# A transformer block on one core: scale before shift, values in partitions by head, probabilities copied by DMA, batched aggregation, and a new order

## The chip, the cores and the metric

The kernel runs on one core of a Trainium2 chip. The metric is the device time of one execution in microseconds; the median of some runs is given. PE is the matmul engine (PEld its weight loads), DVE the vector engine, ACT the scalar engine, POOL GpSimd; SP issues most DMAs. Each engine takes its instructions in program order.

## The reference

One batch, S = 2048 rows, D = 512, 32 heads of 16, bf16.

```python
mod = silu(c) @ w_mod                      # six vectors: sa, ca, ga, sb, cb, gb
h = layernorm(x) * (1 + ca) + sa
q, k, v = heads(h @ wqkv)
# row s sees rows s, s-2, ..., s-14 (8 offsets w, dilation 2; before the start: masked)
logits[s, w] = (q[s] . k[s - 2w]) / 4
o[s] = sum_w softmax(logits)[s, w] * v[s - 2w]
x = x + ga * (o @ wo)
h = layernorm(layernorm(x) * (1 + cb) + sb)
u = gelu(einsum('sd,sf->df', h, w1) + b1)  # an MLP over the rows, F = 1792
x = x + gb * (einsum('df,fs->ds', u, w2) + b2).T
```

## The kernel before

The rows are taken in four chunks of 512 (`build_chunk`), each of four tiles of 128 rows. For a chunk:

- Statistics of each tile (`ln1s`: on DVE `bn_stats` and `bn_aggr`, on ACT two activations that accumulate), `rstd1` on ACT (Ln, Exp), norms `ln1n`, transposes on PE (`tr`), eviction with scale and shift (`hT`), then K, Q and V (`qkvk`, `qkvq`, `qkvv`) and their evictions (`evk`, `evq`, `evv`). Features lie in partitions as (head, group of 4), four dims j along the free axis.
- `qk`: four products on DVE, one for each dim in a group, over 8 offsets and 512 rows (4096 elements a partition). `red` sums groups of four partitions with the matrix `group4` on PE and puts the four row blocks of 128 into four groups of 32 partitions. `max`, `sub`, `exp`, `sum`, `rb`, `smul` are the softmax.
- `a2`: 32 small matmuls with `selB` bring the probabilities to partitions (offset, head); ACT copies them out (`a2ev`).
- `vd`: 16 DMAs a chunk copy the values, shifted, to the same partitions (`vD`, three buffers).
- `pv`: four products on DVE (4096 elements), `pvacc` sums offsets with `stack4` on PE, `oev` evicts on ACT.
- `wo`: output projection with weights scaled by ga (`gmul`, one of four on POOL, three on DVE, after the DMA `bc0` of the row of ga). Where ACT evicts (`x1ev:a`), PE adds x by a matmul with the identity; where DVE does (`x1ev:v`), DVE adds it. Then the statistics `x1sq`, `rstd2`, the norm `t`, `aff` (two DVE products), `ln3s`, `rstd3`, `h3`.

The first MLP matmul contracts over rows: `mlp1_0_*` takes rows 0 to 1023 as soon as `h3_0` to `h3_7` are there and is parked (`park0`); `mlp1_1_*_0` takes rows 1024 to 1535 and `mlp1_1_*_4` the rest. Then `gadd` (DVE), `gelu` (ACT), `gbm` (DVE), the second MLP `mlp2`, `fin` and the stores.

Nothing decides at run time: the list `ORDER` gives the order in which operations are emitted, so each engine's own order, with the engine (`:v` DVE, `:a` ACT, `:g` POOL) and the PSUM slot. Waits follow from the data. PSUM is four slots of two banks. A few warm-up matmuls (`warm`, on the identity) stand at the head. The pieces that the change replaces, or that the steps turn on:

```python
def f_dve():                      # stats, on DVE
    nc.vector.bn_stats(s6, src)
    nc.vector.bn_aggr(mvt, s6)
...
    av = _ap(a2sb[b][:, 0, 0:1], [[C, 2], [0, 4], [1, C]])          # pv
    vv = _ap(vD[vs][:, 4 * (dq % 2), 8:9], [[-8, 2], [PAD + C, 4], [1, C]])
    nc.vector.tensor_tensor(pvb[:, 2 * pp:2 * pp + 2, :, :], av, vv, op=ALU.mult)
```

Of `ORDER`, from the end of chunk 0's softmax on:

```
... smul0 nb1_3_0:v qk1_2 tr2_00:0 qkvv1_0:2 a2_0:1 hT2_0:a ... a2ev0:a ... pv0_0 pv0_1 ... bc0 khalo2 vd1_030 ...
... max1 pv0_3 pv0_2 ... gmul3:g gmul0:v gmul2:v gmul1:v qk2_1 smul1 qk2_0 ... wo1:0 a2_1:2 x1ev1:a a2ev1:a pv1_0 ...
```

Of the kernel before, what the change touches and what calls it, by code (L numbers as in the profile page):

```python
# [13 lines left out]
P = 128  # L14
# [4 lines left out]
PAD = 16  # L19
# [23 lines left out]
gmul3:g gmul0:v gmul2:v gmul1:v qk2_1 smul1 qk2_0 pvacc0_3 qkvv2_2:1 oev0_3:a evv2_0:a evv2_2:a wo1:0 a2_1:2 x1ev1:a
a2ev1:a pv1_0 pv1_1 wo3:3 wo0:1 wo2:0 x1ev3:a x1sq1 x1sq3 x1ev0:a x1ev2:a qkvk2_2:2 pvacc1_0:3 qkvq2_2:1 pvacc1_1
x1sq2 evk2_2:a x1sq0 rstd2_0_0 evq2_2:a pv1_2 nb2_0_0:v pv1_3 t0:v qk2_3 qk2_2 qkvq3_0:0 pvacc1_2:2 pvacc1_3 qkvk3_0:1
t2:a t3:a oev1_1:a evq3_0:a oev1_3:a t1:a wo6:3 wo7:0 wo5:2 evk3_0:a x1ev6:a vhalo2 ld_b1 bc2 ld_w1_0_1 khalo3 bc1
vd2_101 ld_w1_0_2 vd2_000 ld_w1_0_0 vd2_131 vd2_121 vd2_010 vd2_001 vd2_030 vd2_031 ld_w1_0_3 vd2_020 red2_0:1 red2_1
wo4:3 x1sq6 x1ev7:a x1ev5:a x1sq7 x1sq5 x1ev4:a x1sq4 rstd2_1_0 red2_2 red2_3 aff0_0 qk3_1 ln3s0_1:v nb2_1_0:v
ln3s0_3:a max2 ln3s0_0:v ln3s0_2:v qkvv3_2:0 qkvk3_2:2 sub2 t4:a t7:g t6:g t5:g evv3_2:a exp2 rstd3_0_0 evk3_2:a
aff1_0 nb3_0_0:v qkvv3_0:3 biascols:0 sum2 qkvq3_2:2 rb2 h3_3:a evv3_0:a evq3_2:a ln3s1_2:a ln3s1_3:a h3_1:g h3_0:g  # L50
ln3s1_0:v biascols_cp ln3s1_1:v h3_2:v qk3_0 smul2 qk3_2 rstd3_1_0 mlp1_0_30_0:1 mlp1_0_31_0 mlp1_0_10_0:0 mlp1_0_11_0
a2_2:3 red3_0:2 red3_1 a2ev2:a nb3_1_0:v qk3_3 h3_6:a h3_4:a h3_5:a h3_7:v red3_2 mlp1_0_00_0:3 mlp1_0_01_0 red3_3
mlp1_0_00_4 mlp1_0_01_4 mlp1_0_10_4 mlp1_0_11_4 pv2_0 max3 park0_0:a sub3 pvacc2_0:3 vd2_120 vhalo3 ld_w1_0_6 vd2_011
ld_w1_0_4 vd3_030 vd2_110 vd2_021 vd2_100 vd2_130 vd3_001 vd2_111 vd3_031 vd3_000 vd3_011 vd3_110 vd3_020 vd3_010
vd3_021 exp3 pv2_1 mlp1_0_31_4 sum3 pvacc2_1 mlp1_0_30_4 rb3 oev2_1:a park0_3:a pv2_2 smul3 pv2_3 mlp1_0_60_0:2 a2_3:3
mlp1_0_60_4 pvacc2_2:1 vd3_120 vd3_111 vd3_100 vd3_131 vd3_101 vd3_130 ld_w1_1_1 vd3_121 ld_w1_0_5 ld_w1_1_3 ld_w2_0
ld_w1_1_0 bc3 pvacc2_3 mlp1_0_61_0 mlp1_0_61_4 a2ev3:a park0_1:a oev2_3:a wo8:3 wo10:0 wo11:1 x1ev8:a park0_6:a pv3_0
pv3_1 x1ev10:v wo9:3 pvacc3_0:2 x1ev11:v x1ev9:v pv3_2 x1sq10 x1sq8 x1sq11 x1sq9 rstd2_2_0 pvacc3_1 nb2_2_0:v t8:a
t10:a t9:a oev3_1:a t11:v pv3_3 aff2_0 mlp1_0_20_0:0 mlp1_0_21_0 mlp1_0_40_0:1 mlp1_0_41_0 mlp1_0_20_4 mlp1_0_21_4
# [3 lines left out]
ld_w1_1_2 ld_w1_1_5 ld_w1_1_4 ld_w2_2 ld_w2_6 ld_w1_1_6 ld_w2_1 rstd2_3_2 aff3_0 nb2_3_2:v t15:v t14:v aff3_2
park0_5:a ln3s3_1:a ln3s3_0:a rstd3_3_0 ln3s3_3:v ln3s3_2:v nb3_3_0:v rstd3_3_2 h3_13:v h3_12:a nb3_3_2:v h3_15:v
h3_14:v mlp1_1_00_0:0 mlp1_1_10_0:3 mlp1_1_30_0:2 mlp1_1_01_0 mlp1_1_31_0 mlp1_1_11_0 mlp1_1_50_0:1 mlp1_1_51_0
mlp1_1_01_4 mlp1_1_10_4 mlp1_1_00_4 mlp1_1_11_4 xb0 gadd1 gadd0 gelu2 gelu3 mlp1_1_30_4 mlp1_1_31_4 mlp1_1_20_0:3
mlp1_1_51_4 mlp1_1_21_0 mlp1_1_50_4 mlp1_1_21_4 mlp1_1_20_4 mlp1_1_40_0:0 gadd3 gbm3 gelu0 gelu7 gelu6 gelu1 gbm7 gbm2
# [30 lines left out]
class _Graph:  # L98
# [11 lines left out]
    def slot(self, pool):  # L110
        return _Slot(pool)
# [120 lines left out]
def kernel(  # L232
# [14 lines left out]
    WARM=(4, 4, 4, 5, 4),  # L247
# [733 lines left out]
```

## Time and profile before

| what | value |
|---|---|
| median of 3 runs | 198.63 us (198.53 to 199.68) |
| span of the profiled execution | 197.0 us; its own device time is not given, so 1.6 us lie between its span and the median |
| instructions | 3408 |
| busy: PE, DVE, ACT, POOL | 190.1, 153.5, 123.4, 18.0 us |
| granted PE clock | 0.998 |
| DMA | 33.59 MB |

A line of the timeline reads: start, length (both in us), engine, line, operation, output <- inputs, shapes, xcount, and in brackets the idle time of the engine just before and what ended it. All lines carry L184, since a helper records every operation; go by the names. A group reads: busy time, mean ns of one | idle time before them. The length of one instruction includes its way through the engine; the next independent one starts some 0.1 us before it ends, so from start to start is what counts in a full list. PE's lengths overlap: 16 matmuls of 512 columns take 3.6 us, though each is listed with 0.38.

### The profile page before, as it was taken

To read this page: it belongs to the slowest core of one execution; us is meant where nothing else is said; L and a number is where in the kernel's file an instruction comes from. 1 tells how busy PE (TensorE), PEld (TensorE's weight loads), DVE (VectorE), ACT (ScalarE), POOL (GpSimd) and SP (SyncE) were. 2 spreads that over 40 slices of the span, in tenths; PEclk is the share of its full clock that TensorE was granted. 3 is DMA by queue.
4 is the path that set the end of the run, shared out by engine and by line. 5 is a ranking of instruction groups with operands and counts; after the bars stand their busy time and mean duration, and the time that the engine had idled before them with its cause. 6 is when DMAs were issued, how large, how long until landed. Compare 5 with 4: busy or idle time off the path is not lost.

```text
span 197.0 us, 3408 instructions
## 1 busy us (share of the span) xinstructions
PE 190.1 (97%) x1289; PEld 88.2 (45%) x1289; DVE 153.5 (78%) x198; ACT 123.4 (63%) x242; POOL 18.0 (9%) x46
## 2 busy tenths in 40 slices
PE   7889999999999999999999999999999999999994
PEld 2546545445443435433434444444444444444452
DVE  1699989999999999999999999928776127261463
ACT  5498999999999999993769999917541000000000
POOL 7003040090000004300000011000000000000000
PEclk9999999999999999999999999999999999999999
DMA  6999978507994994693999999990000871720112
GB/s 182 369 312 318 302 195 177 120 14 180 171 196 99 270 201 84 187 289 106 174 206 290 234 295 292 292 273 4 0 0 0 229 200 68 199 81 26 57 53 80
DMA packets 45348, 33.59 MB, mean 171 GB/s; under 512 B 5396, under 2 KB 42772, under 8 KB 45332
## 3 DMA queue, kind: packets, MB, share of 16 engines
q1 hardware_dynamic: 44908, 32.82, 67.2%
q10 hardware_dynamic: 424, 0.56, 1.0%
q8 instruction: 10, 0.16, 0.4%
q14 instruction: 6, 0.05, 0.1%
HBM read 22.03 MB, written 2.10 MB: 122 GB/s over the span
## 4 chain that ended last, share of the span: by engine, by line
PE 64%; DVE 12%; DMA 11%; ACT 5%; SPq 3%; issue 2%; ACTq 0%; DVEq 0%
PE ps L184 64%; DMA vD<-v_c 5%; DMA w_q<-in_A_wqkv_dram 4%; SPq L184 3%; DVE pvb L184 3%; DVE prod L184 3%; DMA vD<-in_w_mod_dram 3%; DVE st L184 2%; ACT n_sb L184 1%; DVE h L184 1%; ACT hTb L184 1%; DVE gT L184 1%; ACT v_c L184 1%; DVE ee L184 1%; DVE nm L184 1%
## 5 line engine op out<-in xcount | busy, mean ns | idle before, releaser
L184 DVE TENSOR_TENSOR pvb<-a2sb,vD 128x4096 bf16<-128x4096 bf16 x16 | 36.0, 2284 | 0.2 <-issue 0.2
L184 PE MATMUL ps<-h,wst 128*128 128x512 bf16 x128 | 29.5, 379 | 0.0
L184 DVE TENSOR_TENSOR prod<-q_sb,k_c 128x4096 bf16<-128x4096 bf16 x9 | 20.4, 2285 | 0.1
L184 PEld LDWEIGHTS <-wst 128*128 128x128 bf16 x128 | 12.1, 98 | 16.0 <-issue 1.7
L184 PE MATMUL ps<-gT,vD 128*128 128x512 bf16 x84 | 19.1, 379 | 0.0
L184 PE MATMUL ps<-hTb,w_q 128*128 128x512 bf16 x64 | 15.1, 381 | 1.0 <-DMA w_q<-in_A_wqkv_dram 0.7
L184 DVE TENSOR_TENSOR q_sb<-ps,q_sb 128x512 bf16<-128x512 f32 x8 | 5.4, 687 | 13.6 <-PE ps L184 13.6
L184 PE MATMUL ps<-woq,o_sb 128*128 128x512 bf16 x64 | 15.8, 379 | 0.0
L184 PEld LDWEIGHTS <-w_q 128*128 128x128 bf16 x96 | 9.9, 109 | 12.6 <-issue 2.5
L184 PE MATMUL ps<-hTb,w_v 128*128 128x512 bf16 x64 | 15.0, 380 | 0.0
L184 PE MATMUL ps<-hTb,w_k 128*128 128x512 bf16 x64 | 15.0, 380 | 0.0
L184 DVE TENSOR_TENSOR k_c<-ps,k_c 128x512 bf16<-128x512 f32 (+2 forms) x9 | 5.6, 629 | 11.7 <-PE ps L184 11.7
L184 PEld LDWEIGHTS <-o_sb 128*128 128x128 bf16 x106 | 9.7, 98 | 10.5 <-issue 0.4
L184 PEld LDWEIGHTS <-vD 128*128 128x128 bf16 x116 | 9.2, 97 | 11.4 <-DMA vD<-in_w_mod_dram 1.5
L184 PE MATMUL ps<-gT,pvb 128*128 128x512 bf16 x56 | 12.9, 379 | 0.0
L184 PEld LDWEIGHTS <-w_k 128*128 128x128 bf16 x80 | 8.7, 111 | 8.9 <-issue 0.8
L184 PE MATMUL ps<-gT,prod 128*128 128x512 bf16 x56 | 12.2, 379 | 0.0
L184 PEld LDWEIGHTS <-w_v 128*128 128x128 bf16 x80 | 8.3, 111 | 8.2 <-issue 1.3
L184 ACT ACTIVATE junk<-xx,su 128x512 bf16<-128x512 bf16 x16 | 11.5, 720 | 0.5 <-DVE xx L184 0.2
L184 DVE BATCH_NORM_STATS2 st<-xx 128x6 f32<-128x512 bf16 x11 | 7.4, 671 | 4.7 <-DMA xx<-in_A_x_dram 4.7
L184 ACT ACTIVATE hTb<-ps,sacol,a1col 128x512 bf16<-128x512 bf16 x13 | 9.6, 782 | 0.5 <-PE ps L184 0.5
L184 DVE TENSOR_TENSOR gT<-q_sb,k_c 128x4096 bf16<-128x4096 bf16 x4 | 9.1, 2284 | 0.0
(113 smaller groups left out, 315.1 us busy)
## 6 DMA issues: line engine op xcount, KB each, us to landing
vD<-v_c SPq DMA_DIRECT2D x64, 131.5 KB, 4.6
wst<-in_B_w_dram SPq DMA_DIRECT2D x8, 512.0 KB, 6.1
vD<-in_B_w_dram SPq DMA_DIRECT2D x3, 896.0 KB, 7.3
wst<-in_w_mod_dram SPq DMA_DIRECT2D x4, 512.0 KB, 9.3
prod<-in_B_w_dram SPq DMA_DIRECT2D x2, 896.0 KB, 11.0
pvb<-in_B_w_dram SPq DMA_DIRECT2D x2, 896.0 KB, 8.1
xx<-in_A_x_dram SPq DMA_DIRECT2D x4, 256.0 KB, 4.7
xx<-in_A_x_dram SPq DMA_DIRECT2D x2, 512.0 KB, 7.7
```

The source lines that it names most:

```text
L184: r = fn(*a, **k)
```

## The change

Seven edits, and a new `ORDER` over all:

1. **PSUM** is one tile of eight single banks, and an operation takes one or two neighbouring ones.
2. **Scale first.** The scale vector ca is loaded and multiplied out ahead (`ld_ca0`, `ld_ca1`, `colsa`, `a1_cp`), the shift sa later (`ld_sa`, `colss`, `sa_cp`). In chunk 0 the eviction only scales (`hk`, in two halves of rows), K is computed from that, with the contraction block outermost and in two halves of 256 rows, and the shift comes in as a column at its eviction (`kbias`, `kb_cp`). For Q and V `hadd` adds the shift.
3. **Values by head.** Partition = 4 x head + offset within four; one DMA where there were four (4 a chunk), 526 KB each.
4. **Probabilities by DMA.** `a2` and `a2ev` go; four DMAs a chunk (`a2d`) copy 32 x 1024 elements each, 512 bytes a partition. `group4` serves for `pvacc` too; `stack4` and `selB` go. `red` writes the offsets in another order for it.
5. **`pv`** is two DVE instructions of 2048 elements instead of one of 4096.
6. **Batched aggregation.** `bn_aggr` goes; five small DVE operations (`gather`) do it for a run of tiles whose statistics DVE took. `rstd` needs one Ln a group.
7. **Order and engines.** All four `gmul` go to POOL, 11 instead of 9 `x1ev` to ACT, three of five `warm` groups to the place before `mlp1_0`, and more.

```diff
-            nc.vector.bn_aggr(mvt, s6)
+    def gather(s6, mvt, agt, ops, g0, reads, writes, name):   # for each run of DVE tiles r
+                nc.vector.tensor_tensor(d_, s6[:, r, 1], s6[:, r, 4], op=ALU.subtract)
+                nc.vector.scalar_tensor_tensor(mvt[:, r, 0], d_, -0.5, s6[:, r, 1], op0=ALU.mult, op1=ALU.add)
+                nc.vector.scalar_tensor_tensor(q_, d_, D / 4.0, d_, op0=ALU.mult, op1=ALU.mult)
+                nc.vector.tensor_tensor(q_, q_, s6[:, r, 2], op=ALU.add)
+                nc.vector.tensor_tensor(mvt[:, r, 1], q_, s6[:, r, 5], op=ALU.add)
...
+                        for j in range(4):                                       # qkvk0_{kt}_{g0}
+                            nc.tensor.matmul(bank(sk[j], 0)[:, g0 * P:g1 * P], lhsT=_ap(w_p[1][:, kt, j:j + 1], [[4, P]]),
+                                             rhs=hraw[:, kt, g0 * P:g1 * P], start=(kt == 0), stop=(kt == KT - 1))
...
-                for w4 in range(4):
-                    s0 = PAD - 8 - 2 * w4
-                    src = v_c[b][2 * hfd + dh2::4, :, :].rearrange("h j s -> h (j s)")[:, s0:s0 + nrun]
-                    dst = vD[vs][32 * w4:32 * w4 + 32, 4 * dh2:4 * dh2 + 4, :].rearrange("h j s -> h (j s)")[:, 0:nrun]
+                src = v_c[b][2 * hfd + dh2::4, :, :].rearrange("h j s -> h (j s)")[:, PAD - 8:PAD - 7]
+                src = _ap(src, [[-DIL, 4], [1, nrun]])
+                dst = vD[vs][:, 4 * dh2:4 * dh2 + 4, :].rearrange("p j s -> p (j s)")[:, 0:nrun]
...
-                            nc.tensor.matmul(bank(sa2, jh)[32 * w4:32 * w4 + 32, c0:c0 + SB], ...
+        for jj in range(4):
+            src = ee[b][32 * jj:32 * jj + 32, :, :].rearrange("h (w a) s -> h w (a s)", w=4)
+            dma(a2sb[b][:, jj, :, :].rearrange("p w s -> p (w s)"), src, P * 2 * SB * 2, [("ee", b)], [("a2sb", b, jj)],
+                f"a2d{ch}_{jj}")
...
-                nc.vector.tensor_tensor(pvb[:, 2 * pp:2 * pp + 2, :, :], av, vv, op=ALU.mult)
+                for wp in range(2):
+                    av = _ap(a2sb[b][:, 0, wp, 0:1], [[0, 4], [2 * SB, 4], [1, SB]])
+                    vv = _ap(vD[vs][:, 4 * (dq % 2), 8 - 8 * wp:9 - 8 * wp], [[PAD + C, 4], [SB, 4], [1, SB]])
+                    pv_ = pvb[:, 2 * pp + wp, :, :].rearrange("p d (j s) -> p d j s", s=SB)
+                    nc.vector.tensor_tensor(pv_, av, vv, op=ALU.mult)
```

The new `ORDER` up to the first output projection, cut:

```
consts ld_c ld_x00 ld_x02 ld_ca0 ld_ca1 act_table ln1s1:v ln1s0:v agg1_0_0 ld_wk0 ld_wk2 consts2 warm0:0 rstd1_0_0
cps:0 silu_exp ln1s3:v nb1_0_0:v silu_dve ln1s2:v warm1:1 ld_sa agg1_0_2 ld_b2 ln1n0:a ln1n1:g colsa:0 tr0_00:1 ld_b1
a1_cp:v rstd1_0_2 tr0_10:2 hk0_0:v nb1_0_2:v ln1n3:v hk1_0:a qkvk0_0_0:0345 ln1n2:v qkvk0_1_0 tr0_02 ld_x1a halo0
tr0_12 hk2_0:v colss:6 biascols:7 sc_rep ld_x1b hk3_0:a hk1_2:a sa_cp:a ld_wq qkvk0_2_0 hk0_2:v ln1s4:a ld_wo2 ld_x2
qkvk0_3_0 hk3_2:a hk2_2:v ln1s5:v hadd0:v ln1s7:v kbias:1 ld_wv ln1s6:v qkvk0_0_2 ... agg1_1_0 ... rstd1_1_0 ...
... evq0_1:a ... qk0_1 qk0_0 qkvv0_2:4 ... agg1_2_0 qk0_2 qk0_3 ... ln1n9:g ln1n8:g ln1s14:v ... max0 sub0 ... exp0 ...
... qk1_0 qk1_1 smul0 agg1_3_0 vd0_00 ... qk1_3 ... qk1_2 ld_w1_0_1 ... a2d0_3 a2d0_1 a2d0_2 a2d0_0 vd0_01 ...
... pv0_0 max1 ... pv0_1 ... rb1 ... pv0_2 smul1 ... pv0_3 ... qk2_2 a2d1_2 a2d1_0 a2d1_3 khalo3 a2d1_1 ...
... gmul0:g qk2_0 pvacc0_3 oev0_3:a pv1_0 vd1_10 gmul2:g gmul3:g gmul1:g qkvv2_0:0 vhalo2 ... wo3:2 wo2:3
wo0:0 pvacc1_0:4 wo1:1 qkvk3_0:6 x1ev3:a x1sq3 x1ev2:a ... rstd2_0_0 pv1_1 pvacc1_1 red2_0:0 pv1_2 nb2_0_0:v pv1_3 ...
```

More of the change, by code (lines that the diff above doesn't have):

```diff
@@ L43 @@
[L43 to L47, printed above, removed]
@@ L63 @@
[L63 to L67, printed above, removed]
@@ L291 @@
     ee = [T([P, NW, SB], BF, f"ee{i}") for i in range(2)]
-    a2sb = [T([P, 2, C], BF, f"a2sb{i}") for i in range(2)]
+    a2sb = [T([P, 4, 2, SB], BF, f"a2sb{i}") for i in range(2)]
     nm = [T([P, SB], BF, f"nm{i}") for i in range(2)]
@@ L334 @@
     nb = [small([P, TPC], f"nb{k}") for k in range(3)]
+    ag = [small([P, 2, TPC], f"ag{k}") for k in range(2)]
     su2 = small([P, TPC], "su2")
@@ new lines, in f_sa_act, with f_kb @@
+    def f_sa_act():
+        nc.scalar.activation(sabf[:], bank(sl_m[0], 0)[:, 0:KT], ACT.Identity)
+        nc.scalar.activation(sacol[:], bank(sl_m[0], 0)[:, 0:KT], ACT.Identity)
+    G.add_any([("act", 0.34, f_sa_act), ("dve", 0.2, f_sa_dve)], reads=[sl_m[0]], writes=["sacol"], name="sa_cp",
+              lat=0.1, use=[sl_m[0]])
+    sl_kb = G.slot("ps", 1)
+    def f_kb():
+        for j in range(4):
+            for kt in range(KT):
+                nc.tensor.matmul(bank(sl_kb, 0)[:, j:j + 1], lhsT=_ap(w_p[1][:, kt, j:j + 1], [[4, P]]),
+                                 rhs=sabf[:, kt:kt + 1], start=(kt == 0), stop=(kt == KT - 1), skip_group_check=True)
```

392 lines of the change are left out of this document (214 added, 178 removed).

## The prediction

> **What bounds the kernel now.** I read the page first (busy shares, the 40 slices, the chain), then the stages, then the timeline of DVE and PE around the hand-overs.
>
> ```profile
> span 197.0 us, 3408 instructions
> PE 190.1 (97%) x1289; PEld 88.2 (45%) x1289; DVE 153.5 (78%) x198; ACT 123.4 (63%) x242; POOL 18.0 (9%) x46
> DVE  1699989999999999999999999928776127261463
> PEclk9999999999999999999999999999999999999999
> PE 64%; DVE 12%; DMA 11%; ACT 5%; SPq 3%; issue 2%; ACTq 0%; DVEq 0%
> ```
>
> PE at 97% looks like the only bound. The stages say more: DVE is full until 127 us as well.
>
> ```profile
> 50.00:60.00 10.00, 10.00 (x83) 4.57 (x83) 10.00 (x6) 9.94 (x21) 0.00 (x0) 1.00 1.00 177
> ```
>
> The columns after the stage's length are PE, PEld, DVE, ACT and POOL, then clock, DMA share and GB/s. What decides is the hand-over to the second half of the first MLP matmul (`mlp1_1_*_4`), which needs `h3_12` to `h3_15`:
>
> ```profile
> 16.67 4.49 DVE L184 TENSOR_TENSOR prod<-q_sb,k_c 128x4096 bf16<-128x4096 bf16 x2
> 126.64 1.08 DVE L184 TENSOR_SCALAR h<-h,mv,rs 128x512 bf16<-128x512 bf16 x3
> 126.86 0.80 ACT L184 ACTIVATE h<-h,nb,rs 128x512 bf16<-128x512 bf16 x1
> 128.28 6.21 PE L184 MATMUL ps<-h,wst 128*128 128x512 bf16 x28
> 192.71 1.38 PE L184 MATMUL ps<-gT,o_sb 128*128 128x512 bf16 x16
> ```
>
> DVE multiplies its first q and k at 16.67 and writes the last normalized row (`h3_14`) at about 127.7, ACT its own at 127.66; PE asks for them at 128.28. So PE and DVE arrive together, 0.6 us apart. From 128.28 PE works without a gap to 194.1, and the rest (last sums and stores) ends the span at 197.0. A change that shortens only PE's work before 128 gains nothing beyond those 0.6 us; one that lengthens DVE's by more moves the end nearly one for one. I charge about 0.2 us of the slack for the hand-over: **end moves = move of DVE's list minus 0.4**.
>
> **PE's part.** The selector matmuls `a2_*` go, replaced by DMAs.
>
> ```profile
> 36.58 0.42 PE L184 MATMUL ps<-ee,selB 64*32 64x128 bf16 x32 [0.39 <-DVE ee L184]
> 36.93 1.92 PE L184 MATMUL ps<-hTb,w_v 128*128 128x512 bf16 x8
> 10.40 3.61 PE L184 MATMUL ps<-hTb,w_k 128*128 128x512 bf16 x16
> 14.70 3.65 PE L184 MATMUL ps<-hTb,w_q 128*128 128x512 bf16 x16 [0.69 <-DMA w_q<-in_A_wqkv_dram]
> 10.24 0.62 ACT L184 ACTIVATE junk<-xx 128x512 bf16<-128x512 bf16 x1
> 11.83 0.63 ACT L184 ACTIVATE junk<-xx 128x512 bf16<-128x512 bf16 x1
> ```
>
> 32 of them take 0.35 us (36.58 to 36.93), four times 1.4 us. Eleven residual rows are added on PE instead of nine: 2 x 0.22 = +0.4 (3.61/16 each). The first key matmul of chunk 0 now needs only the scale half of the table and two row tiles. From the last rows (5.66, below) to that matmul (10.40) it takes 4.7 us now; the same chain from the first rows (3.45) puts it near 8.2. But the other half of K waits for rows 2 and 3, and its last operand `hk3_2` stands on ACT behind the statistic `ln1s4`, which takes 1.6 us there (10.24 to 11.83), so K ends near 13.7 where it ends at 14.0 now. The wait for w_q (0.69) can go: by the issue order 3.1 MB lie up to its end instead of 3.6. PE gains 0.3 to 2.1 us at the head; the 16 tiny `kbias` matmuls and twice as many, half as long key matmuls lie in PE's early waits, and the eight warm-up matmuls that move fill an idle place. PE arrives 1.3 to 3.1 us early, and waits for DVE.
>
> ```profile
> L184 ACT ACTIVATE a2sb<-ps 128x1024 bf16<-128x1024 f32 x4 | 4.1, 1020 | 0.3 <-PE ps L184 0.3
> ```
>
> ACT is full in the middle (9.94 of 10 above) but gets lighter there: four `a2ev` go, 4.1 us; `hk`, `hadd` and an eviction come at the head. I cost that at nothing; were ACT late, `evq0_1` would hold the first product, by one eviction of 0.6 us. PSUM in single banks costs nothing by itself: it only lets the new order place things.
>
> **DVE's part, early.** From the first rows to the first q-k product DVE has this list in the new order: 10 statistics, 3 gathers, 3 norms, 4 half evictions `hk`, 3 `hadd`, one key eviction and some eight tiny ones.
>
> ```profile
> 3.45 0.69 DVE L184 BATCH_NORM_STATS2 st<-xx 128x6 f32<-128x512 bf16 x1 [3.45 <-DMA xx<-in_A_x_dram]
> 5.66 0.69 DVE L184 BATCH_NORM_STATS2 st<-xx 128x6 f32<-128x512 bf16 x1 [1.26 <-DMA xx<-in_A_x_dram]
> 75.68 0.18 DVE L184 BATCH_NORM_AGGREGATE mv<-st 128x2 f32<-128x6 f32 x1
> 75.78 0.66 DVE L184 BATCH_NORM_STATS2 st<-h 128x6 f32<-128x512 bf16 x1
> 76.48 0.18 DVE L184 BATCH_NORM_AGGREGATE mv<-st 128x2 f32<-128x6 f32 x1
> 36.45 0.16 DVE L184 SCALAR_TENSOR_TENSOR nb<-mv,rs 128x4 f32<-128x4 f32 x1
> 36.52 2.28 DVE L184 TENSOR_TENSOR gT<-q_sb,k_c 128x4096 bf16<-128x4096 bf16 x1
> 7.28 1.43 DVE L184 TENSOR_SCALAR n_sb<-xx,mv,rs 128x512 bf16<-128x512 bf16 x4
> 9.81 1.45 DVE L184 TENSOR_SCALAR hTb<-ps,a1col,sacol 128x512 bf16<-128x512 bf16 x3 [1.10 <-PE ps L184]
> ```
>
> A statistic with its aggregation takes 0.80 from start to start (75.68 to 76.48); the aggregation alone costs 0.10, and a dependent one makes the statistic wait out its full length. Without it I take 0.62, an estimate (0.69 less the 0.08 by which independent work overlaps). The **gather** is five tiny operations, three of them on the result of the one before. A tiny one costs 0.07 where nothing depends on it (36.45 to 36.52) and 0.16 to 0.18 in full. Ends: 5 x 0.08 = 0.40 and 5 x 0.18 = 0.90; taken 3 x 0.17 + 2 x 0.08 = 0.67, nearest to the dependent ones. Then 10 x 0.62 + 3 x 0.67 + 3 x 0.36 + 4 x 0.25 + 3 x 0.36 + 0.6 + 0.8 = 12.8, plus about 1.0 of waits for rows and transposes (now 1.26 and 1.10), from 3.45: 17.2. **+0.5** against 16.67, from -0.4 (cheap gather, no waits) to +1.6 (dear gather, waits as now).
>
> **DVE's part, late.** From the first product to `h3_14`:
>
> ```profile
> L184 DVE TENSOR_TENSOR pvb<-a2sb,vD 128x4096 bf16<-128x4096 bf16 x16 | 36.0, 2284 | 0.2 <-issue 0.2
> L184 DVE TENSOR_TENSOR h<-h,ab_bc 128x2048 bf16<-128x2048 bf16 x3 | 3.6, 1214 | 0.0
> 54.67 6.69 DVE L184 TENSOR_TENSOR pvb<-a2sb,vD 128x4096 bf16<-128x4096 bf16 x3
> 48.66 1.09 DVE L184 TENSOR_TENSOR woq<-woq,ga_bc 128x512 bf16<-128x512 bf16 x3
> 104.03 0.68 DVE L184 SCALAR_TENSOR_TENSOR xx<-ps,xx 128x512 bf16<-128x512 f32 x1
> 104.80 0.69 DVE L184 SCALAR_TENSOR_TENSOR xx<-ps,xx 128x512 bf16<-128x512 f32 x1
> ```
>
> Each `pv` becomes two instructions of 2048: 2 x (1.21 - 0.08) = 2.27 against 2.20 (6.69 for three), x16 = +1.2 (0 to +1.4). Gathers 6 x 0.67 = +4.0 (2.4 to 5.4). Statistics 12 x 0.80 to 11 x 0.62 = -2.8. Two norms more of chunk 2 +0.7, one more `t` +0.3, two residual evictions fewer 2 x 0.77 (104.03 to 104.80) = -1.5, three `gmul` moved to POOL -1.0. Sum **+0.9**, from -1.9 to +2.4. The batched aggregation thus saves 21 small operations and pays 45.
>
> **Waits that replace the removed work.** The probabilities now go `smul` to four SP-issued DMAs to `pv`.
>
> ```profile
> 36.04 0.62 SPq L184 DMA_DIRECT2D ga_bc<-mrow  x1
> 38.97 5.25 POOL L184 TENSOR_TENSOR woq<-woq,ga_bc 128x512 bf16<-128x512 bf16 x1 [10.80 <-DMA ga_bc<-mrow]
> k_c<-k_c SPq DMA_DIRECT2D x3, 16.0 KB, 2.3
> vD<-v_c SPq DMA_DIRECT2D x64, 131.5 KB, 4.6
> 38.72 4.49 DVE L184 TENSOR_TENSOR pvb<-a2sb,vD 128x4096 bf16<-128x4096 bf16 x2
> 43.13 1.22 DVE L184 TENSOR_REDUCE nm<-ps 128x128 bf16<-128x1024 f32 x1
> ```
>
> Four issues of about 0.62 and a landing of 2.3 (small copy) to 4.6 (busy queue): 4.8 to 7.1 us. DVE's work between `smul` and the first `pv` is, by chunk, a gather and two products (5.1), a `pv` and two products (6.7), two products with small work and the maximum (7.0), and two `pv` (4.5). Waits 0 to 2.0, 0.4, 0.1, 2.6: I take **+0.6** of 0 to +4, since the queue is lighter (16 value copies instead of 64). Behind them on SP's queue stand the next value copies and w1 loads; the copies are needed one `pv` (2.3) later, the loads tens of us later.
>
> **The four `gmul` on POOL** are the dangerous edit. The one that POOL does now took 5.25 us: it sat under two `pv` products (38.72 to 43.2) and ended 1.1 us after they did, under the maximum, which reads PSUM. So POOL gets on only when DVE leaves its two-input products, and needs about 1.1 us each time. Now all of `wo0` to `wo3` wait for four such windows between the landing of `ga_bc` (about 33) and 53, while DVE runs q-k, `max1` and `pv`. One window is sure (`max1`), one likely (the gather before `qk1_3`); others are gaps where DVE waits for `rb` or a DMA. I take +1.2: they get in, and DVE waits out the rest of a 1.1 us operation about once. Ends 0 and +7.4 (second rival).
>
> **Sum.** 0.5 + 0.9 + 0.6 + 1.2 = 3.2, less 0.4: the end moves +2.8. Span 197.0 to 199.8. The median of the runs, 198.63, is 1.6 above the profiled span, and I keep that: **201.4 us**. The case's own range is 200.7 to 204.5.
>
> **Rivals.** *DVE wins at every open price, PE becomes the bound (faster).* Gather 0.40, split `pv` free, no waits: DVE -0.4 - 1.9 = -2.3, and PE, 2.1 + 1.4 - 0.4 = 3.1 early, is ready. The end moves -2.7: 195.9. For it: DVE's two early idles (1.26, 1.10) can be filled. Against: 45 tiny operations in dependent chains. It decides at a gather below 0.45 with the first product before 16.3. Chance 0.22.
>
> *POOL starved (slower).* If one to three `gmul` are left when `max1` ends, PE stands at `wo3`, behind which `pvacc1_0` is queued; `pv1_2` needs the buffer that `pvacc1_0` frees. DVE then runs dry after `pv1_1`, about 60 us, and only then does POOL get on:
>
> ```profile
> L184 PE MATMUL ps<-pvb,stack 128*32 128x512 bf16 x128 | 9.0, 383 | 0.1
> ```
>
> 1.1 to 3.3 of POOL, three `wo` of five matmuls at 0.22, a `pvacc` 0.56 (9.0/16), hand-overs 0.3: 5.2 to 7.4, say 6.3 for two left. 0.5 + 0.9 + 0.6 + 6.3 - 0.4 = 7.9: 206.5. Against it: DVE has small gaps in which POOL may be let in. Chance 0.20. The Trainium skill, GPSIMD Engine Reference, section 8 (Key points), says that POOL contends for SBUF with VectorE instructions that have two SBUF inputs. By that rule q-k, `pv` and `smul` all shut POOL out, which is this rival; the trace agrees in the one case it has (5.25 us). In this rival PE would stand for some 8 us, and the Trainium skill, TensorE: Matmul & The Clock Gate, Part 1, says a window of about 3.4 us idle halves the clock until such a window is busy again; no row here shows that, and by it an estimated 1.7 us would come on top.
>
> *Gains and losses cancel.* Gather 0.45, `pv` +0.6, waits 0.6, the `gmul` in DVE's gaps: early 0.1, late -1.0, in sum about -0.7, with the unsteady rest -0.5 to +1.5: 197.5 to 200.5, centre 198.6. Chance 0.20. My forecast has 0.38.
>
> **How the numbers follow.** About 1% (2 us) is what a measurement of this kernel tells from no change, so 196.6 to 200.6 is "same". Faster is the first rival, 0.22; same the third, 0.20; slower the forecast and the starved POOL, 0.58. The range 195.5 to 207.0 leaves out about half of either outer case.
>
> **What would show it.** Right: first q-k product at 17 or later; tiny DVE operations of 0.15 in chains of five; `h3_14` near 130.5 and an idle of PE of 1 to 3 us before `mlp1_1_*_4`; POOL's `woq` operations several us long. Starved POOL: PE idle over 5 us before the first `woq` matmul, DVE idle before a `pvb` product near 60. Wrong: PE without a gap from 20 on and `h3_14` before 127, or DVE idle behind DMA `a2sb` for more than 3 us in all.

## The result, and the profile after

| | us |
|---|---|
| before, median of the runs beside it | 198.53 (197.97 to 199.68) |
| after, median of 5 runs | 208.13 (207.34 to 210.33) |
| ratio, with its 95% interval | 1.0492 (1.0429 to 1.0556) |
| forecast | 201.4 (195.5 to 207.0) |

The change makes the kernel 9.6 us slower. The direction was forecast, the size (+2.8) was not: the result lies above the range. Here and below, executions more than 1.5% above the fastest of the same kernel are left out of the ratios, so that a ratio need not be the quotient of two medians. The profile shown is of an execution that took 210.33, the longest of the five. Lines of the page of after (span and instructions, busy times, DVE and the granted PE clock in 40 slices of 5.2 us):

```profile
span 208.4 us, 3205 instructions
PE 194.8 (93%) x1190; PEld 91.9 (44%) x1190; DVE 162.4 (78%) x239; ACT 119.1 (57%) x236; POOL 20.9 (10%) x44
DVE  2777998999999999999998899996875251643551
PEclk9757999987999999999999999999999999999999
```

DVE is busy nine microseconds longer (162.4 against 153.5; 3.6 of them are the lengthened gather below), and PE's clock, at full speed in every slice before, is low at two places. The stages show both places (columns: PE, PEld, DVE, ACT, POOL, clock, DMA share, GB/s):

```profile
9.00:12.00 3.00, 2.84 (x27) 2.36 (x27) 1.35 (x6) 0.59 (x3) 0.00 (x0) 0.50 1.12 334
12.00:15.00 3.00, 3.00 (x39) 2.37 (x37) 2.93 (x9) 2.97 (x10) 0.00 (x0) 0.50 1.09 321
15.00:18.00 3.00, 3.00 (x17) 2.06 (x14) 1.47 (x8) 0.88 (x4) 1.50 (x3) 0.50 1.13 275
40.00:50.00 10.00, 7.43 (x42) 2.69 (x43) 9.65 (x10) 7.19 (x11) 2.67 (x3) 0.83 0.33 112
```

**The head.** From the timeline of PE and DVE of after: PE stands (is idle) 2.16 us with the warm-ups gone, the clock falls to half, the first 8 of the 32 key matmuls of 256 columns take 1.87 us (1.03 in e1 below, at full clock), DVE waits 1.33 us for the last of them, and the first q-k product starts at 20.50 (before 16.67, forecast 17.2).

```profile
7.17 0.54 PE L185 MATMUL ps<-sc,vD 128*128 128x1 bf16 x16 [2.16 <-DVE sc L185]
9.16 1.87 PE L185 MATMUL ps<-gT,w_k 128*128 128x256 bf16 x8 [0.78 <-DVE gT L185]
17.89 0.75 DVE L185 TENSOR_SCALAR k_c<-ps,kbcol 128x512 bf16<-128x512 f32 x1 [1.33 <-PE ps L185]
20.50 4.48 DVE L185 TENSOR_TENSOR prod<-q_sb,k_c 128x4096 bf16<-128x4096 bf16 x2
```

**The middle.** The four `gmul` on POOL, the gather `agg1_3_0` on DVE at the same time, and those who wait for it on ACT and PE:

```profile
37.62 5.05 POOL L185 TENSOR_TENSOR woq<-woq,ga_bc 128x512 bf16<-128x512 bf16 x4 [5.47 <-issue]
38.24 1.11 DVE L185 TENSOR_TENSOR ag<-st 128x1 f32<-128x1 f32 x1
39.39 1.08 DVE L185 SCALAR_TENSOR_TENSOR mv<-ag,st 128x1 f32<-128x1 f32 x1
40.39 0.15 DVE L185 SCALAR_TENSOR_TENSOR ag<-ag 128x1 f32<-128x1 f32 x1
40.57 1.01 DVE L185 TENSOR_TENSOR ag<-ag,st 128x1 f32<-128x1 f32 x1
41.61 1.07 DVE L185 TENSOR_TENSOR mv<-ag,st 128x1 f32<-128x1 f32 x1
42.60 2.28 DVE L185 TENSOR_TENSOR h<-q_sb,k_c 128x4096 bf16<-128x4096 bf16 x1
42.72 0.30 ACT L185 ACTIVATE lv<-mv,epscol 128x4 f32<-128x4 f32 x1 [3.57 <-DVE mv L185]
44.03 0.38 PE L185 MATMUL ps<-hTb,w_k 128*128 128x512 bf16 x1 [2.20 <-ACT hTb L185]
```

Five operations on one number per partition take 4.36 us (38.24 to 42.60). An undisturbed gather takes 0.75 from start to start:

```profile
14.58 0.17 DVE L185 TENSOR_TENSOR ag<-st 128x3 f32<-128x3 f32 x1
...
15.33 0.61 DVE L185 TENSOR_SCALAR hTb<-gT,sacol 128x512 bf16<-128x512 bf16 x2
```

Four of the five are longer by 0.9 each, 3.6 us, which fits one for each POOL product. Behind the gather `rstd1_3_0` waits on ACT, behind that, in ACT's order, the evictions `hT2`, and so PE.

**The end.** DVE's last norm and the second half of the first MLP matmul, 11.8 and 11.2 us later than before:

```profile
138.78 0.73 DVE L185 TENSOR_SCALAR h<-h,mv,rs 128x512 bf16<-128x512 bf16 x2 [0.20 <-ACT rs L185]
139.51 8.58 PE L185 MATMUL ps<-h,wst 128*128 128x512 bf16 x39 [0.50 <-ACT h L185]
```

### The profile page after: what moved, and what is told of

Same layout as the page of the kernel before. It is cut to its first block, busy times and chain, and to the rows that moved or that the text cites. A ratio compares the mean times of both kernels' runs of the same rounds, so it can differ in the third digit from the quotient of the medians.

```text
span 208.4 us, 3205 instructions
## 1 busy us (share of the span) xinstructions
PE 194.8 (93%) x1190; PEld 91.9 (44%) x1190; DVE 162.4 (78%) x239; ACT 119.1 (57%) x236; POOL 20.9 (10%) x44
## 4 chain that ended last, share of the span: by engine, by line
PE 53%; DVE 23%; ACT 17%; issue 3%; DMA 1%; POOL 0%; DVEq 0%; ACTq 0%; POOLq 0%
PE ps L185 53%; DVE h L185 5%; DVE prod L185 5%; ACT junk L185 4%; DVE st L185 4%; DVE ag L185 2%; ACT q_sb L185 2%; ACT hTb L185 2%; DVE mv L185 2%; ACT k_c L185 2%; ACT xx L185 2%; DVE pvb L185 2%; ACT h L185 2%; DMA xx<-in_A_x_dram 1%; DVE gT L185 1%
## 5 line engine op out<-in xcount | busy, mean ns | idle before, releaser
L185 DVE TENSOR_TENSOR pvb<-a2sb,vD 128x2048 bf16<-128x2048 bf16 x32 | 37.1, 1217 | 0.9 <-PE ps L185 0.8
L185 PEld LDWEIGHTS <-wst 128*128 128x128 bf16 x128 | 12.3, 98 | 17.2 <-issue 3.4
L185 PEld LDWEIGHTS <-w_k 128*128 128x128 bf16 x112 | 12.0, 122 | 13.4 <-issue 5.7
L185 PE MATMUL ps<-woq,o_sb 128*128 128x512 bf16 x64 | 16.3, 380 | 0.0
L185 PE MATMUL ps<-hTb,w_k 128*128 128x512 bf16 x48 | 12.5, 400 | 2.6 <-ACT hTb L185 2.5
L185 PE MATMUL ps<-gT,prod 128*128 128x512 bf16 x56 | 12.9, 379 | 0.0
L185 ACT ACTIVATE o_sb<-ps 128x1024 bf16<-128x1024 f32 x8 | 8.2, 1023 | 3.9 <-PE ps L185 3.9
L185 PEld LDWEIGHTS <-group 128*32 128x32 bf16 x256 | 5.5, 98 | 10.9 <-issue 7.4
```

Of the source, the lines that this page charges most:

```text
L185: r = fn(*a, **k)
```

## The experiments

The time of a kernel is its median, the ratio is to the kernel before run on the same chip beside it.

| kernel | us | ratio (95%) |
|---|---|---|
| e1_warm_head | 207.17 | 1.0442 (1.0407 to 1.0476) |
| e2_gmul_dve | 205.12 | 1.0346 (1.0306 to 1.0385) |
| e3_warm_gmul | 203.58 | 1.0265 (1.0239 to 1.0291) |
| e4_aggr_back | 201.02 | 1.0137 (1.0112 to 1.0162) |
| e5_pv_one | 200.37 | 1.0114 (1.0084 to 1.0143) |
| e6_pv_one_nb3 | 200.46 | 1.0114 (1.0085 to 1.0144) |
| e7_aggr_gmul_pool | 203.87 | 1.0287 (1.0251 to 1.0324) |
| b1_before_cold_head | 199.42 | 1.0021 (0.9973 to 1.0070) |
| b2_before_gmul_pool | 200.12 | 1.0098 (1.0080 to 1.0116) |
| b3_before_two_evictions | 199.00 | 0.9999 (0.9960 to 1.0038) |
| h1_old_order_after_head | 209.75 | 1.0556 (1.0491 to 1.0622) |
| h2_old_order_two_evictions | 207.63 | 1.0488 (1.0431 to 1.0545) |

### The row scalings on POOL

**e2: the change, with all four `gmul` on DVE.**

```diff
-gmul0:g qk2_0 pvacc0_3 oev0_3:a pv1_0 vd1_10 gmul2:g gmul3:g gmul1:g qkvv2_0:0
+gmul0:v gmul2:v gmul3:v gmul1:v qk2_0 pvacc0_3 oev0_3:a pv1_0 vd1_10 qkvv2_0:0
```

> The changed kernel with the four gmul on DVE, just ahead of qk2_0, instead of POOL. Theory (POOL's four products get SBUF in the gaps between the dependent tiny operations of the gather and hold DVE there for 3.7 us): the gather before qk1_3 takes 0.75 instead of 4.4 us, PE has no 3 us gap near 42 us and no clock of 0.66 to 0.77 after it; DVE pays 1.4 us for the four: 2.3 to 3.5 us less, 204.5 to 206. Rival (that time is DVE's slack, other waits take its place): within 1 us of 208.1.

Measured: 3.0 us less than the change, as the theory had it. In its trace the same gather starts at 36.11 and the next product at 36.83, so it takes 0.72 us again, and PE no longer stands before the keys.

```profile
36.11 0.15 DVE L185 TENSOR_TENSOR ag<-st 128x1 f32<-128x1 f32 x1
36.83 2.29 DVE L185 TENSOR_TENSOR h<-q_sb,k_c 128x4096 bf16<-128x4096 bf16 x1
```

**e7: POOL keeps the four, but there is no gather for them to fall on** (the aggregation for each tile back, as in e4 below). My theory was that the gather's gaps were the trouble.

```diff
-gmul0:v gmul2:v gmul3:v gmul1:v qk2_0 pvacc0_3 ...         # e4
+gmul0:g qk2_0 pvacc0_3 ... gmul2:g gmul3:g gmul1:g         # e7
```

> The changed kernel with warm-ups and aggregation per tile back, but with the four row scalings on POOL where the change has them. Theory (POOL's products run only when DVE is between two instructions, and the gather's dependent tiny instructions were such places, at about 1.05 us each): without the gather POOL's group takes longer than the 5.05 us of the change, DVE loses under 1.5 us to it, and the time is 201 to 202, that is within 1 us of the 201.02 with the scalings on DVE. Rival one (a starved POOL is late for the output projection): PE stands over 3 us before the first product with wo, time 203 to 206. Rival two (DVE loses about 1 us for each POOL product wherever it runs): 204 to 205.

Measured: 203.87, 2.9 us over e4, so the theory falls, and the rival with about 1 us of DVE for each POOL product holds (its 204 to 205 was a little high). Timeline of POOL and DVE, and last the pair of value products of e4:

```profile
34.03 10.16 POOL L185 TENSOR_TENSOR woq<-woq,ga_bc 128x512 bf16<-128x512 bf16 x4 [5.08 <-issue]
34.88 2.97 DVE L185 TENSOR_TENSOR h<-q_sb,k_c 128x4096 bf16<-128x4096 bf16 x1 [0.19 <-ACT q_sb L185]
37.77 1.11 DVE L185 SCALAR_TENSOR_TENSOR nb<-mv,rs 128x4 f32<-128x4 f32 x1
41.01 4.27 DVE L185 TENSOR_TENSOR pvb<-a2sb,vD 128x2048 bf16<-128x2048 bf16 x2
51.59 0.69 DVE L185 TENSOR_TENSOR ee<-ee,rb 128x1024 bf16<-128x1024 bf16 x1 [0.65 <-ACT rb L185]
39.56 2.36 DVE L185 TENSOR_TENSOR pvb<-a2sb,vD 128x2048 bf16<-128x2048 bf16 x2
```

A q-k product is 2.97 instead of 2.29, a tiny factor 1.11 instead of 0.15, a pair of value products 4.27 instead of 2.36: 0.7 + 1.0 + 1.9 = 3.6 us for four. e4 spends 1.3 us of DVE on the four scalings (52.57 to 53.91 in its timeline), so 2.2 us are net. The two executions of e7 with a mean clock of 0.998 and more lose about that (203.16 and 203.46 against 201.0); the two with 0.992 lose 3.3 and 3.6. The profile is of one of these: PE stands 0.67, 0.97 and 0.74 us behind the late products, its clock is 0.50 from 48 to 50 us, and DVE waits for `rb` (51.59 above; e4 has no such wait). POOL has the four done at 44.2, and the output projection starts at 58.6, so POOL isn't starved; DVE pays.

**b2: the kernel before, with four on POOL instead of one.**

```diff
-gmul3:g gmul0:v gmul2:v gmul1:v qk2_1 smul1 qk2_0 ...
+gmul3:g gmul0:g gmul2:g gmul1:g qk2_1 smul1 qk2_0 ...
```

> The kernel before, with all four row scalings on POOL at the same place in the order and nothing else changed (one is on POOL there already and took 4.23 us). Theory (POOL gets in only between DVE's instructions, here long products with no dependent tiny ones): DVE saves 3 x 0.7 us of its own list, but the four on POOL take 10 us or more and the output projection of chunk 0 waits for them: 200 to 203. Rival (there is place enough): within 0.5 us of the kernel before or up to 1 us faster.

Measured: 1.9 us slower. Timeline of POOL, DVE and PE, and last the same two value products of the kernel before:

```profile
40.58 10.65 POOL L184 TENSOR_TENSOR woq<-woq,ga_bc 128x512 bf16<-128x512 bf16 x4 [12.97 <-DMA ga_bc<-mrow]
43.83 6.39 DVE L184 TENSOR_TENSOR pvb<-a2sb,vD 128x4096 bf16<-128x4096 bf16 x2
50.14 3.25 DVE L184 TENSOR_TENSOR prod<-q_sb,k_c 128x4096 bf16<-128x4096 bf16 x1
50.27 1.05 PE L184 MATMUL ps<-pvb,stack 128*32 128x512 bf16 x16 [1.68 <-DVE pvb L184]
44.26 4.48 DVE L184 TENSOR_TENSOR pvb<-a2sb,vD 128x4096 bf16<-128x4096 bf16 x2
```

Two value products take 6.39 instead of 4.48, a q-k product 3.25 instead of 2.28: 2.9 us for three POOL products. The fourth cost nothing: as the one that POOL already did before, it fell under the maximum, which reads PSUM (POOL's first product ends at 43.8, the maximum runs from 42.69 and takes its usual 1.22). DVE saved 1.0 by giving three away (48.66 to 49.67 in the kernel before), so 1.9 net, and that is the time measured. The size came out as the theory had it, its reason (the output projection waits) did not: PE waited for DVE's value products. The 4.23 us in the expectation are only the part of the one POOL product that lies behind 40 us; it took 5.25.

### The clock at the head

**e1: nine warm-up matmuls more behind `warm1`. e3: e1 and e2 together.**

```diff
-silu_dve ln1s2:v warm1:1 ld_sa          WARM=(4, 4, 2, 3, 3)
+silu_dve ln1s2:v warm1:1 warm5:1 ld_sa  WARM=(4, 4, 2, 3, 3, 9)
```

> The changed kernel with nine more warm-up matmuls on PE between warm1 and the scale columns, where PE stands idle from 5.0 to 7.2 us. Theory (cold clock: with 8 warm-ups instead of 21 at the head PE's granted clock falls to 0.5 from 9 to 18 us, the key matmuls take twice as long, and DVE's first q-k product comes at 20.5): clock 1.0 up to 20 us, K done by about 15, first product at 17.2 to 17.8, time 2.5 to 3.3 us less, about 205. Rival (DVE's own list at the head is what is longer; the clock only shows that PE waits): first product within 0.5 us of 20.5, time within 1 us of 208.1.

> Both edits: warm-ups at the head and gmul on DVE. Theory (two separate losses on DVE's one full list): they add up, 5 to 6.8 us less, 201.5 to 203. Rival (one hides the other, since PE or ACT then sets the pace): no more than the larger of the two alone, about 205.

Measured: 1.0 us less for e1 alone, though the intervals of e1 and of the change overlap, and 1.5 for e3 against e2, where they don't. Both are under their theories (2.5 to 3.3 for e1, 5 to 6.8 for both edits; 4.5 measured). In e1 the clock is 1.00 in all stages up to 40 us, and the first product starts at 18.11, 2.4 earlier than in the profile of the change. That execution took 210.33 and the profiled one of e1 207.14, so there the gain at the head arrives in full. The median of the change is lower because its executions differ in how cold they are: their mean clocks lie between 0.967 (210.33 us) and 0.999 (207.34), though not in strict order with the times, while the four of e1 lie within 0.4 us. And POOL takes its share all the same: e1 is 3.6 us over e3, which differs from it only by the four `gmul`. Timeline of DVE, and the stage, of e1:

```profile
18.11 4.48 DVE L185 TENSOR_TENSOR prod<-q_sb,k_c 128x4096 bf16<-128x4096 bf16 x2
34.50 1.65 DVE L185 TENSOR_TENSOR ee<-ee,rb 128x1024 bf16<-128x1024 bf16 x1
36.07 1.11 DVE L185 TENSOR_TENSOR ag<-st 128x1 f32<-128x1 f32 x1
40.00:50.00 10.00, 8.64 (x53) 3.14 (x54) 9.72 (x8) 8.54 (x12) 0.00 (x0) 0.83 0.52 174
```

PE stands behind the delayed gather here too (2.21 us), and the clock is 0.83 in this stage, as in the change; e1 leaves that loss as it is.

**b1: the kernel before with 8 warm-ups instead of 21.**

```diff
-    WARM=(4, 4, 4, 5, 4),
+    WARM=(4, 4, 0, 0, 0),
```

> The kernel before with 8 warm-up matmuls at the head instead of 21, nothing else changed. Theory (in the changed kernel a gap of some 2 us on PE in the first 7 us let the granted clock fall to 0.50 for 3 to 9 us, and the key projection took twice as long; filling the gap gave 1.0 us there): PE stands 2 us or more before 7 us, the clock shows 0.5 to 0.85 in the stages from 6 to 18 us, the first q-k product starts 1 to 4 us after 16.67, and the time grows by 1.0 to 3.5 us. Rival (PE has slack enough in the kernel before, or the gap is too short here): no more than 0.4 us.

Measured: no difference that could be told (1.0021); the interval reaches to some 1.4 us, so a small cost isn't excluded. A stage and the first product:

```profile
9.00:12.00 3.00, 2.28 (x12) 1.32 (x11) 2.08 (x5) 2.46 (x6) 0.00 (x0) 0.56 1.10 349
17.20 4.49 DVE L184 TENSOR_TENSOR prod<-q_sb,k_c 128x4096 bf16<-128x4096 bf16 x2 [0.61 <-ACT q_sb L184]
```

The clock falls here too, to 0.50 from 9 to 11 us, and the first product is 0.5 us later; the rival holds. PE's stands are shorter here (0.82 and 0.89 us, for loads), and from 12 us on the clock is at 1.00 again. So in this trace the missing warm-ups alone are not dear; they were dearer together with the new head, where PE waits longer.

### Aggregation

**e4: e3 with `bn_aggr` for each tile back and no gather** (and so, on ACT, the Ln again split by the engine that took the statistics; not in the cut below).

```diff
+            nc.vector.bn_aggr(mvt, s6)
...
-        add("dve", 0.35, f, reads=reads, writes=writes, name=name, lat=0.08)      # the five operations of gather
+        add("dve", 0.0, lambda: None, reads=reads, writes=writes, name=name, lat=0.0)
```

> Both edits, and the batched aggregation undone: an aggregation for each tile on DVE again and the Ln split by engine on ACT, no gather. Theory (the gather's nine chains of 0.74 us cost more than the 21 aggregations at 0.17 to 0.19 that they replace, and DVE's list sets the end): 2 to 3 us below the run with both edits, about 200. Rival (the gather lies in DVE's slack, or the split roots on ACT cost as much): within 1 us of it.

Measured: 2.6 us less. Both kernels take 21 statistics on DVE, so this compares nine gathers at 0.75 with 21 aggregations: 6.75 against 21 x 0.18 = 3.8 would be 3.0 on DVE's list.

### One value product instead of two

**e5: e4 with the probabilities stored so that one instruction covers both halves.**

```diff
-    a2sb = [T([P, 4, 2, SB], BF, ...)]          dma(a2sb[b][:, jj, :, :]..., src, ...)
+    a2sb = [T([P, 2, C], BF, ...)]              dma(a2sb[b][:, :, jj * SB:(jj + 1) * SB], src, ...)
-                for wp in range(2): ...  nc.vector.tensor_tensor(pv_, av, vv, op=ALU.mult)
+                nc.vector.tensor_tensor(pvb[:, 2 * pp:2 * pp + 2, :, :], av, vv, op=ALU.mult)
```

> Compared with the kernel with warm-ups, row scalings on DVE and aggregation per tile back (201.02): the probabilities land in an order that lets one product cover both offsets, 16 products of 128x4096 in place of 32 of 128x2048; nothing else changes. Theory (DVE's list sets the end, so a DVE saving moves it nearly one for one): a pair took 2.32 us against 2.25 us for one, 16 x 0.07 = 1.1 us, so 199.9 (199.6 to 200.3). Rival (PE's own waits set the end by now): 200.7 to 201.1. A third way: the shorter runs of the four copies (256 bytes) make them land later and DVE waits for them: above 201.2.

Groups of the change and of e5 (busy, mean ns of one | idle before):

```profile
L185 DVE TENSOR_TENSOR pvb<-a2sb,vD 128x2048 bf16<-128x2048 bf16 x32 | 37.1, 1217 | 0.9 <-PE ps L185 0.8
L185 DVE TENSOR_TENSOR pvb<-a2sb,vD 128x4096 bf16<-128x4096 bf16 x16 | 36.0, 2284 | 1.2 <-PE ps L185 0.7 <-DMA a2sb<-ee 0.5
```

DVE's 1.1 us are saved, the medians differ by 0.65 (the ratios by 0.0023, some 0.5 us), and the intervals of the two ratios overlap: the direction fits, the size at the end is not settled.

### What is left, and the order

e5 has undone the POOL, clock, gather and split-product terms and is still 2.1 us over the kernel before. DVE from its first statistic to `h3_14`, before and e5:

```profile
3.45:127.70 124.25, 121.70 (x964) 56.84 (x964) 118.82 (x145) 111.62 (x227) 15.74 (x30) 1.00 0.89 216
3.60:129.55 125.95, 123.07 (x877) 59.84 (x876) 120.21 (x150) 108.10 (x227) 14.10 (x20) 1.00 0.84 241
```

DVE is busy 1.4 us longer and idle 0.3 longer. The groups of the head (first line before, the others e5):

```profile
L184 DVE TENSOR_SCALAR hTb<-ps,a1col,sacol 128x512 bf16<-128x512 bf16 x3 | 1.4, 538 | 1.1 <-PE ps L184 1.1
L185 DVE TENSOR_SCALAR gT<-ps,a1col 128x256 bf16<-128x256 bf16 x4 | 1.3, 347 | 0.8 <-PE ps L185 0.7
L185 DVE TENSOR_SCALAR hTb<-gT,sacol 128x512 bf16<-128x512 bf16 x3 | 0.9, 333 | 0.0
L185 DVE TENSOR_SCALAR k_c<-ps,kbcol 128x512 bf16<-128x512 f32 x1 | 0.7, 744 | 0.0
```

Scale first, add the shift later and evict a key on DVE: 2.9 us where 1.4 stood. The two residual sums moved to ACT take 1.5 off, but DVE waits 2.1 us behind PE and the copies in that stretch (timeline of DVE, e5):

```profile
91.49 4.49 DVE L185 TENSOR_TENSOR pvb<-a2sb,vD 128x4096 bf16<-128x4096 bf16 x2 [0.54 <-DMA a2sb<-ee]
101.68 4.49 DVE L185 TENSOR_TENSOR pvb<-a2sb,vD 128x4096 bf16<-128x4096 bf16 x2 [0.69 <-PE ps L185]
107.02 0.69 DVE L185 SCALAR_TENSOR_TENSOR xx<-ps,xx 128x512 bf16<-128x512 f32 x1 [0.85 <-PE ps L185]
```

**b3: the kernel before, with those two residual sums on ACT.**

```diff
-pv3_1 x1ev10:v wo9:3 pvacc3_0:2 x1ev11:v ...
+pv3_1 x1ev10:a wo9:3 pvacc3_0:2 x1ev11:a ...
```

> The kernel before, with two residual sums of chunk 2 evicted by ACT instead of DVE (the change has this among its new engines), nothing else. It takes 2 x 0.77 us from DVE's list and gives PE two matmuls of 0.22. Theory of the prediction (DVE and PE reach the second half of the first MLP matmul within 0.6 us of each other, so that DVE's gain alone is worth nothing): -0.4 to +0.5 us. Rival (DVE alone sets the end, as a copy of this edit on the kernel with the old order suggests, where it gave 2.1 us): -0.9 to -1.6 us.

Measured: 0.9999 (within 0.8 us either way). 1.5 us off DVE's list alone are worth nothing there that could be told. Its timeline shows where they go:

```profile
109.88 0.69 DVE L184 SCALAR_TENSOR_TENSOR xx<-ps,xx 128x512 bf16<-128x512 f32 x1 [1.90 <-PE ps L184]
```

DVE now waits 1.90 us for PE before the one residual sum of the chunk that it keeps; the kernel before has no such wait. In this execution (202.99) PE stood 2.80 us at the head for a load of w_mod, the clock was 0.50 from 9 to 15 us, and the first product started at 21.35, with all 21 warm-ups in place; from 20 us on the clock is 1.00.

**e6: e5 with the second norm of chunk 1 ahead of a q-k product and of an eviction.**

```diff
-ln3s1_3:a evv3_2:a agg3_1_0 qk3_3 rstd3_1_0 h3_1:g nb3_1_0:v warm4:2 h3_6:v ... h3_5:v
+ln3s1_3:a agg3_1_0 rstd3_1_0 evv3_2:a h3_1:g nb3_1_0:v warm4:2 h3_6:v h3_5:v qk3_3 ...
```

> The kernel before it in this batch, with the normalization factors of chunk 1's second norm computed on ACT ahead of the eviction of v, and that norm's rows on DVE ahead of the last q-k product of chunk 3. Theory (two waits of PE near 82 and 91, 0.96 and 0.58 us, come from DVE and POOL rows that are late by one q-k product of 2.2 us; DVE in turn waits 0.93 us for PE near 108): both fall, 0.5 to 0.9 us less than the kernel with one product. Rival (the last softmax gets late by the same amount and gives it back at the first value products of chunk 2 or 3): no difference within 0.3 us.

Measured: no difference (both 1.0114). The rival holds: DVE's waits between 88 and 108 us are 0.16, 0.54, 0.69 and 0.85 us in e5 and 0.78, 0.19, 0.56 and 0.85 in e6, so what is gained at one turns up at another.

**h1: the head and the data path of e5, with the order and engines of the kernel before from the second product on. h2: h1 with `x1ev10` and `x1ev11` on ACT.**

```diff
-... smul0 agg1_3_0 vd0_00 ... qk1_3 ... qk1_2 ld_w1_0_1 ... a2d0_3 a2d0_1 a2d0_2 a2d0_0 ... pv0_0 max1 ...
+... smul0 nb1_3_0:v qk1_2 tr2_00:0 qkvv1_0:4 a2d0_0 a2d0_1 a2d0_2 a2d0_3 hT2_0:a ... pv0_0 pv0_1 ...
```

> The kernel with one value product per step (200.37) up to the first two q-k products; from there on the order and the engines of the kernel before, with the four copies of the probabilities where its selector matmuls stood. So the change's head and data path, the old order. Theory (what is left over the kernel before, 2.1 us, is half head and half the new order, in which the second norm of chunk 1 and the last softmaxes arrive late on PE and DVE waits 2.1 us for PE and copies between 90 and 108): 198.8 to 199.6. Rival (the copies of the probabilities cost a wait of DVE of 0.5 to 1 us each in the old order, which had eviction time instead): 200.5 to 203, with DVE idle behind DMA a2sb. A third way (all of the rest is head): 200.0 to 200.6.

> The same with two residual sums of chunk 2 on ACT instead of DVE (2 x 0.69 us), which the change has too. Theory (DVE's list sets the end up to 128 us, ACT stands idle at 100 to 103): 0.6 to 1.4 us less than the kernel before it. Rival (PE is late there by as much, so that DVE only waits longer): within 0.3 us.

Measured: 209.75 and 207.63. My theory that the new order costs about 1 us falls clearly; the rival holds and is larger than it said. Timeline of DVE, h2:

```profile
42.37 5.46 DVE L185 TENSOR_TENSOR pvb<-a2sb,vD 128x4096 bf16<-128x4096 bf16 x2 [2.09 <-DMA a2sb<-ee]
61.69 6.70 DVE L185 TENSOR_TENSOR pvb<-a2sb,vD 128x4096 bf16<-128x4096 bf16 x3 [2.32 <-DMA v_c<-v_c]
110.18 4.49 DVE L185 TENSOR_TENSOR pvb<-a2sb,vD 128x4096 bf16<-128x4096 bf16 x2 [3.95 <-DMA a2sb<-ee]
```

In this order DVE waits 2.1, 2.3 and 4.0 us for copies (the middle one for values, the others for probabilities), 8.4 us in all, and h2 is some 7.3 us over e5; in the trace of the change no such wait is listed. So the new order belongs to the copies by DMA. The first pair of value products, 5.46 instead of 4.49, is one more case of a POOL product beside DVE: delayed by the copies, the pair now meets the one `gmul` on POOL (43.61 to 45.68). That h2 is 2.1 us under h1, by the edit that gave nothing on the kernel before, is not shown to be the edit's worth: the intervals overlap, and in the profile of h1 the clock is 0.90 and 0.76 between 40 and 60 us, long before the two sums, where that of h2 is 1.00. No version here beats the kernel before.

## Why the prediction was right and wrong

| step | forecast | measured |
|---|---|---|
| four `gmul` on POOL (+1.2, and -1.0 on DVE) | +0.2 | +3.0 (change against e2), +3.6 (e1 against e3), +2.9 (e7 against e4) |
| gathers for aggregations (9 x 0.67 - 21 x 0.18) | +2.2 | +2.6 (e3 against e4) |
| `pv` in two | +1.2 | about +0.5 to +0.7, not settled (e4 against e5) |
| warm-ups moved ("fill an idle place") | 0 | +1.5 (e3 against e2); +1.0, not settled (e1) |
| all the rest, less the slack of 0.4 | -0.8 | +2.1 (e5 against before) |
| sum, with +3.0 for the first | +2.8 | +9 to +10 (9.6 measured) |

**Right.** DVE's list sets the end, PE arrives with it (b3), and a longer list moves the end nearly one for one: `h3_14` is 1.9 us later in e5 and the MLP matmul 1.3. Of the signs that were named, the late first product and the chains of 0.15 are there; the idle of PE of 1 to 3 us before `mlp1_1_*_4` (0.50, under **The end**) and POOL operations of several us (four in 5.05) are not. The gather's 0.67 was 0.75, and "saves 21 small operations and pays 45" was the right account. The split `pv` cost DVE 1.1 of the 1.2. The copies were hidden, within the 0 to 4 given for them.

**"The four `gmul` on POOL": the size.** I had read that POOL needs about 1.1 us for itself each time, but then let DVE wait "about once" and called the gather a window. It is no window: a tiny operation there takes 1.1 us instead of 0.15. In every case seen here DVE pays 0.7 to 1.0 us for each POOL product, beside a tiny operation, a q-k product or a value product, unless that falls under the maximum; the single one of the kernel before did, and so looked free. Four such payments, 3.6 us, stand where the sum had one. Less the 1.3 that DVE saves, that is about 2.2, what e7 loses at a full clock; the rest goes with PE's stands behind the late DVE and the low clock after them. The price was within my ends (0 to 7.4), and I chose near the wrong one.

**The starved POOL did not occur.** Its time, 206.5, is nearer to the result than the forecast, but that is luck, for its reason is not there: POOL was done at 42.7, and PE asked for the scaled weights at 62.4; the stand of PE (2.20 us) lay behind the gather. Section 8 (Key points) of the GPSIMD Engine Reference in the Trainium skill, that POOL contends with DVE instructions that have two SBUF inputs, agrees with the rows; reading it as "POOL is shut out" was my mistake. The skill's Trainium Architecture — The Big Picture, What this means for kernel authors, calls the shared port pair an exclusive lock and not a split of bandwidth; the rows, 0.15 to 1.1 us, agree with that as well.

**"PE's part": the idle place.** The warm-ups that moved were not idle filling; with them gone PE stood 2.16 us, and the first key matmuls took nearly twice as long (1.87 against 1.03). That step had no term for it. It also counted eight that move, where thirteen leave the head and eight stand later. The remark on the clock in the prediction hung on a later stand of PE and named a 3.4 us idle window (the Trainium skill, TensorE: Matmul & The Clock Gate, Part 1); here a stand of 2.16 us in the head and one of 2.20 at 44 us were enough, in e7 three of 0.67 to 0.97 us in a row, and the low clock at the head lasted 9 us in the profile of the change and 3 in that of e2.

**The rest.** "DVE's part, early" came out 0.9 short: the first product starts at 18.1 even with a warm clock (e1), not 17.2, since the first rows are there at 3.68 instead of 3.45 and the list itself takes 13.5 us instead of 12.8. "Two residual evictions fewer, -1.5" came off DVE's busy time but not off the end: between 90 and 108 us DVE waits 2.1 us in e5. I took every microsecond off DVE's list as won, although I had said that PE arrives at the same time. Another 0.4 is the fourth `gmul`, which DVE does in e5 and did not before. These pieces are not a sum of the 2.1. This part is read from the traces; no run isolates the head's evictions.

## What to carry to other kernels

A product moved from a full DVE to POOL isn't free, and isn't slow only on POOL: count for each most of the time that POOL needs for it as lost on DVE, unless it falls under a DVE instruction like the maximum here, whose input lies in PSUM. Before removing filler matmuls at the head, look how long PE will stand there: with stands under 0.9 us it cost nothing that could be told (b1), with one of 2.3 us it cost 1.5 us (e3 against e2). Where two engines reach the end together, work taken off one of them may be worth nothing (b3), while work put on one counts nearly in full.

## What the runs showed of the hardware

- A POOL product of two 128 x 512 operands took 1.14 us at the least and lengthened the DVE instruction beside it by 0.7 to 1.0 us: 0.15 to 1.11 (a 128x1 difference), 2.28 to 3.25 (a q-k product), 4.49 to 5.46 (a pair of value products beside one POOL product, h2). Under the maximum, with its input in PSUM, DVE lost nothing (1.22 us as always, in the kernel before and in b2).
- PE's granted clock fell to 0.50 after a stand of 2.16 us with thin work around it (1.2 us busy of the 3 from 6 to 9) and stayed there for 9 us in the profile of the change; in e2, after 2.30 us, for 3 us (8 to 11). It fell to 0.50 without any stand of 1 us too: from 9 to 11 us in b1 (stands of 0.82 and 0.89) and from 48 to 50 us in e7 (0.67, 0.97 and 0.74). It differed from run to run of one kernel (mean clocks 0.967 to 0.999), and with all 21 warm-ups in place it was 0.50 from 9 to 15 us in the profile of b3, behind a late load.
- A DVE operation on 128x1 to 128x4 values takes 0.07 us from start to start where the next one does not depend on it and 0.18 to 0.20 where it does (one gather 0.75); `bn_aggr` costs 0.10 to 0.18, so that one gather has to replace more than four aggregations to gain.
